# Decays kept in the chunk's frame, with query decays on GpSimd and a listed order: a retention, mixing and gated kernel

## The chip, the cores and the metric

The kernel runs on one core of a Trainium2 chip. The metric is the device time of one execution in microseconds; below 381.7 us stands for the kernel before. A core has TensorE (PE in the profile) for matrix products into PSUM, VectorE (DVE), ScalarE (ACT) and GpSimd (POOL) for work on elements, SyncE (SP), which here only issues transfers, and DMA engines between HBM and SBUF, the core's own memory. PSUM has eight banks of 512 float32 words in each of 128 partitions. Each engine works through its own list of instructions in order and waits at semaphores for the others.

## What is computed

Three layers follow each other on batch 2, sequence 768. The first is retention with 8 heads of 64, a state that decays by gamma at each step:

```python
gamma = 1.0 - 2.0 ** (-5.0 - np.arange(H, dtype=np.float32))
for t in range(S):
    state = gamma[None, :, None, None] * state + np.einsum('bhd,bhe->bhde', k[:, :, t], v[:, :, t])
    y[:, :, t] = scale * np.einsum('bhd,bhde->bhe', q[:, :, t], state)
```

The second takes its result as x (768 tokens of 512 features) and mixes tokens with two 768 x 768 matrices:

```python
theta = x @ w_theta
zr, zi = x * np.cos(theta), x * np.sin(theta)
u = x + einsum('ts,bsd->btd', w_tok_r, zr) + einsum('ts,bsd->btd', w_tok_i, zi)
x = u + np.maximum(u @ w_ch, 0.0)
```

The third is a gated layer: h = gelu(x @ w_in), a normalized half of it mixed over tokens by w_sg, multiplied into the other half, and projected back by w_out, with x added.

## The kernel before

The sequence is cut into chunks of 128 tokens: 6 for each batch, 12 in all, numbered i, with c the number within the batch. In `retention(i)` PE makes the scores of keys and queries of a chunk (8 small products), DVE multiplies them by the causal mask, PE makes the outer products of keys and values (8), which DVE adds to a running state, and the attend: state times query, and values times masked scores, into one PSUM bank. Decays are taken apart into powers. Values are multiplied by gamma to the minus t, with t counted from the start of the sequence (`dk`, one column for each chunk and head; ACT for the first eight chunks, DVE for the other four). The result is multiplied by gamma to the t, divided by the root of 64 (`dq`, one table of 256 KB for each chunk, loaded each time). DVE does that on the way out of PSUM, at L554. With these powers the state itself needs no decay.

All wide products are made in float32r in three terms: a number is split into a large part (ACT, a copy that rounds, L310) and the remainder (DVE, a subtraction, L316), and `terms3` issues large by large, remainder by large, large by remainder, for each of the pieces that are summed. Weights come as 1 MB blocks of float64 bits, which ACT (one pass, L369) and DVE (a shift and two combines, L378 and L389) turn into float32 ahead of the split. They land in one of two `raw` tiles.

`theta(i)` makes x @ w_theta in two halves with one weight block each, brings the angle into range, takes sine and cosine on ACT, transposes x with PE (`turn`, L648) and multiplies (L656) into the tile z, which is split too. `mix_main` and `mix_rest` are the token-mixing products. `channels`, `up_v`, `up_u`, `gate_tile` and `finish` follow once both batches are mixed.

Nothing is issued where it stands. Each piece of work becomes an `Op` with an engine, a duration by a formula, what it reads and writes, and a due time. `Plan.schedule` then builds the order greedily: of the work that could start first on an engine, the one with the smallest due time, with tiles and banks handed out as they come free. In the beginning PE has little to do, and up to ninety optional `keep_warm` operations, each one product of the identity matrix with itself, are taken where PE would otherwise stand idle.

All loads are issued by SP:

```python
dma(512, lambda: nc.sync.dma_start(out=ap(load[i, 0]), in_=qkv[b, c, 0]), ...)   # L413, queries and keys
dma(512, lambda: nc.sync.dma_start(out=ap(load[i, 1]), in_=qkv[b, c, 1]), ...)   # L424, keys and values
dma(256, lambda: nc.sync.dma_start(out=ap(dq), in_=dqs[c]), ...)                 # L485, query decays
```

They share eight semaphores in turn, so the issue of one transfer waits until the one eight places before it has landed.

Of the kernel before, what the change touches and what calls it, by code (L numbers as in the profile page):

```python
# [10 lines left out]
F32 = mybir.dt.float32  # L11
# [11 lines left out]
N = B * NCH  # L23

# [36 lines left out]
class Plan:  # L61
# [3 lines left out]
    BEGIN = {"PE": 5.2, "ACT": 2.0, "DVE": 2.0, "POOL": 1.3, "SP": 0.7}  # L65
# [28 lines left out]
    def schedule(self, look):  # L94


        engines = {o.eng: self.BEGIN.get(o.eng, 0.0) for o in self.ops}

        free = {of: [0.0] * n for of, n in self.room.items()}
        rank, level = {}, {}  # L100
        for k, o in enumerate(self.ops):
            o.missing, o.out = len(o.deps), []
            level[o] = max([o.lev, *(level[d] for d in o.deps)])
            rank[o] = k
            for d in o.deps:
                d.out.append(o)
        for o in self.ops:

            if o.eng == "SP" and o.out and not o.deps:
                level[o] = min(level[x] for x in o.out)  # L110
        for k, o in enumerate(sorted(self.ops, key=lambda o: (level[o], rank[o]))):
            o.pos = k
        use = {of: np.zeros(len(self.ops) + 1, np.int64) for of in self.room}
        for b in {b for o in self.ops for b in o.bufs}:
            b.todo = sorted(u.pos for u in b.users)
            b.first = b.todo[0]
            use[b.of][b.first : b.todo[-1] + 1] += 1
        for of, u in use.items():
            assert u.max() <= self.room[of], f"{of}: {u.max()} at {int(u.argmax())}"
        ready = {e: [] for e in engines}  # L120
        for o in self.ops:
            if not o.missing:
                ready[o.eng].append(o)
        state = {"port": 0.0, "dma": 2.1, "first": 0}
        done = [False] * (len(self.ops) + 1)

        def earliest(o):
            t = max(engines[o.eng], o.at, o.prio - (C["PA"] if o.eng == "PE" else C["AHEAD"]))
            if o.port:
                t = max(t, state["port"])  # L130
            o.spots = []
            more = {}
            for b in o.bufs:
                if b.base is not None:
                    continue
                n = more[b.of] = more.get(b.of, 0) + 1
# [1063 lines left out]
```

## Time and profile before

| | |
|---|---|
| median of 3 runs | 381.7 us (381.68 to 381.8) |
| span of the profiled execution | 381.1 us |
| PE busy | 374.7 us, 98% |
| DVE, ACT, POOL busy | 274.0, 175.0, 4.3 us |
| DMA | 41.96 MB, 110 GB/s over the span |
| TensorE's granted clock | 0.999 in the mean |

The profile is of one execution, whose span from the first to the last instruction is 381.1 us; the measured time holds 0.6 us more. A busy PE means that some product is under way. It does not tell whether the product is of use, and products overlap, so a mean duration is longer than the step from one to the next. Where an engine stood idle, the row says how long and which event ended it.

### The profile page before, as it was taken

The numbers are of one execution on the slowest core, as the hardware profiler recorded it, in microseconds if no ns is written. First come the engines' busy times: TensorE is split into PE (matmuls) and PEld (weight loads), VectorE is DVE, ScalarE is ACT, GpSimd is POOL, SyncE is SP. The second block draws the span as 40 slices with busy tenths as digits, with TensorE's granted clock in tenths as the row PEclk, the third lists the DMA queues.
The fourth block names the chain that finished last, engine by engine and source line by source line (L and its number), as shares of the span: only waits on it lengthen the run. The fifth ranks groups of instructions, "written<-read, shape, count | busy, mean of one in ns | idle before, by whom it ended". The sixth has DMA issues, their size and how long they took to land.

```text
span 381.1 us, 5873 instructions
## 1 busy us (share of the span) xinstructions
PE 374.7 (98%) x2422; PEld 318.4 (84%) x2422; DVE 274.0 (72%) x408; ACT 175.0 (46%) x292; POOL 4.3 (1%) x10
## 2 busy tenths in 40 slices
PE   7999999999999999999999999999999999999996
PEld 7877888878988978788998888888888888998885
DVE  1798999997977597869816685899899864544222
ACT  3677988563345335465313443595775711110000
POOL 1000000000000000003000000000000000000000
PEclk9999999999999999999999999999999999999999
DMA  7999553453435603029000160000000000000223
GB/s 258 411 407 407 208 191 110 144 223 132 165 114 192 248 2 113 0 101 352 4 2 2 31 244 2 1 0 0 2 0 1 2 1 0 2 2 35 103 89 106
DMA packets 11931, 41.96 MB, mean 110 GB/s; under 512 B 1536, under 2 KB 2560, under 8 KB 9472
## 3 DMA queue, kind: packets, MB, share of 16 engines
q1 hardware_dynamic: 11904, 41.58, 29.5%
q8 instruction: 19, 0.31, 0.3%
q14 instruction: 8, 0.07, 0.0%
HBM read 38.43 MB, written 3.15 MB: 109 GB/s over the span
## 4 chain that ended last, share of the span: by engine, by line
PE 93%; DMA 5%; SPq 0%; DVE 0%; issue 0%
PE b L290 92%; DMA b<-qkv 5%; PE b L648 1%; DVE b L1027 0%; SPq L424 0%; SPq L441 0%; SPq L413 0%
## 5 line engine op out<-in xcount | busy, mean ns | idle before, releaser
L290 PE MATMUL b<-b,b 128*128 128x512 f32 (+2 forms) x1788 | 332.6, 352 | 0.0
L290 PEld LDWEIGHTS b<-b,b 128*128 128x128 f32 (+1 forms) x1788 | 277.5, 183 | 47.0 <-issue 2.4
L310 ACT ACTIVATE b<-b 128x1024 fp32r<-128x1024 f32 (+1 forms) x64 | 53.2, 859 | 66.7 <-DVE b L975 38.2
L316 DVE TENSOR_TENSOR b<-b,b 128x1024 fp32r<-128x1024 f32 (+1 forms) x64 | 59.3, 955 | 9.7 <-ACT b L310 9.5
L389 DVE SCALAR_TENSOR_TENSOR b<-b 128x1024 int32<-128x1024 int32 x38 | 46.5, 1224 | 1.5 <-ACT b L369 0.5
L310 ACT ACTIVATE b<-xa 128x512 fp32r<-128x512 f32 x24 | 14.6, 626 | 22.9 <-DVE xa L777 9.9
L369 ACT ACTIVATE b<-b 128x1024 f32<-128x1024 f32 x19 | 21.8, 1155 | 3.6 <-DMA b<-wts 3.6
L290 PEld LDWEIGHTS b<-b 64*128 64x128 f32 (+1 forms) x352 | 17.3, 164 | 7.0 <-issue 2.8
L290 PE MATMUL b<-b 64*128 64x128 f32 (+1 forms) x352 | 20.5, 258 | 2.1 <-DMA b<-qkv 2.1
L457 DVE TENSOR_TENSOR b<-b,causal 128x512 f32<-128x512 f32 x24 | 15.7, 684 | 8.2 <-PE b L290 8.2
L316 DVE TENSOR_TENSOR b<-xa,b 128x512 fp32r<-128x512 f32 x24 | 16.2, 687 | 6.2 <-ACT b L310 6.0
L789 ACT ACTIVATE b<-b 128x512 f32<-128x512 f32 x24 | 13.8, 590 | 14.7 <-PE b L290 14.7
L475 ACT ACTIVATE b<-b,dk 128x64 f32<-128x64 f32 x64 | 16.1, 336 | 8.7 <-DMA b<-qkv 8.7
L968 DVE SCALAR_TENSOR_TENSOR b<-b,gcol,brow 128x512 f32<-128x512 f32 x12 | 9.0, 751 | 12.7 <-PE b L290 12.7
L813 DVE SCALAR_TENSOR_TENSOR b<-b,b 128x512 f32<-128x512 f32 x24 | 15.9, 678 | 2.9 <-ACT b L807 2.8
L807 ACT ACTIVATE b<-b 128x512 f32<-128x512 f32 x24 | 14.7, 629 | 6.2 <-DVE b L797 6.1
L797 DVE SCALAR_TENSOR_TENSOR b<-b,b 128x512 f32<-128x512 f32 x24 | 15.5, 672 | 1.9 <-ACT b L789 1.9
L604 ACT ACTIVATE b<-b 128x512 int32<-128x512 f32 x12 | 7.1, 594 | 19.9 <-PE b L290 19.9
L990 DVE TENSOR_TENSOR b<-b,xa 128x512 f32<-128x512 f32 x8 | 5.5, 690 | 14.2 <-PE b L290 14.2
L310 ACT ACTIVATE b<-xb 128x512 fp32r<-128x512 f32 x12 | 7.3, 628 | 17.5 <-DVE xb L735 9.9
L378 DVE TENSOR_SCALAR b<-b 128x1024 int32<-128x1024 int32 x19 | 13.1, 691 | 2.9 <-DMA b<-wts 2.7
L656 DVE TENSOR_TENSOR b<-b,b 128x1024 f32<-128x1024 f32 x12 | 14.6, 1220 | 0.8 <-ACT b L639 0.4
(51 smaller groups left out, 168.9 us busy)
## 6 DMA issues: line engine op xcount, KB each, us to landing
b<-wts SPq DMA_DIRECT2D x19, 1024.0 KB, 5.0
b<-qkv SPq DMA_DIRECT2D x24, 512.0 KB, 8.4
b<-dqs SPq DMA_DIRECT2D x12, 256.0 KB, 9.2
out<-b SPq DMA_DIRECT2D x11, 256.0 KB, 2.0
b<-wsg SPq DMA_DIRECT2D x9, 256.0 KB, 7.5
brow<-bvec SPq DMA_DIRECT2D x1, 384.0 KB, 7.7
out<-b SPq DMA_DIRECT2D x2, 128.0 KB, 1.7
dk<-decays SPq DMA_DIRECT2D x1, 24.0 KB, 3.4
```

Source lines behind the costliest of these rows:

```text
L290: nc.tensor.matmul(out=o, lhsT=l, rhs=r, start=start, stop=stop)
L310: act(words, lambda: A.activation(out=hi(), in_=src(), func=AF.Copy), prio=prio, r=r, **k)
L316: lambda: E.tensor_tensor(out=lo(), in0=src(), in1=hi().bitcast(F32), op=ALU.subtract),
L369: lambda: A.activation(out=words(1).bitcast(F32), in_=words(1).bitcast(F32), func=AF.Copy, scale=REBIAS),
L389: lambda scalar=scalar, op=op: V.scalar_tensor_tensor(out=words(0), in0=words(1), scalar=scalar, in1=words(0), op0=op, op1=ALU.bitwise_or,),
L457: V.tensor_tensor(out=ap(at[i])[:, h * 512 : (h + 1) * 512].rearrange("p (n t) -> p n t", n=NP), in0=ap(sc[h]).rearrange("p (n t) -> p n t ...
L475: A.activation(out=v, in_=v, func=AF.Copy, scale=dk[:, c, h : h + 1])
L656: V.tensor_tensor(out=z2, in0=ap(tp)[:, None, :].to_broadcast([P, 2, 512]), in1=z2, op=ALU.mult)
L789: lambda: A.activation(out=ap(s), in_=ap(t), func=AF.Square),
L797: lambda: V.scalar_tensor_tensor(out=ap(s), in0=ap(s), scalar=1.0 / GA, in1=ap(t), op0=ALU.add, op1=ALU.mult),
L807: lambda: A.activation(out=ap(s), in_=ap(s), func=AF.Tanh, scale=GA * GC),
L813: lambda: V.scalar_tensor_tensor(out=ap(o), in0=ap(s), scalar=1.0, in1=ap(t), op0=ALU.add, op1=ALU.mult),
```

## The change

Decays move into the frame of the chunk, with t counted from 1 to 128 in each. One table `dec` holds the query decays (512 columns), the value decays of the 8 heads and gamma to the 128 for the state. It is loaded once, and the twelve loads of `dqs` and the one of `dk` are gone. Queries are now multiplied by their decays ahead of the scores, in place: by DVE for chunk 0, by GpSimd for the other eleven (`weigh`). The state is multiplied by gamma to the 128 from chunk to chunk: in the copy itself after a batch's first chunk, by GpSimd after the four next (`shrink`). The result leaves PSUM without a multiply. ACT copies it to x and takes the large part, both from the bank, and DVE takes the remainder from the bank. All value decays are on ACT.

PSUM is one tile of eight banks, and the mask is one DVE instruction over two banks. Three weight blocks (both of theta, and the third of the token weights) land in the space of x tiles that are still empty, instead of in a `raw` tile. Chunk 0's keys and values are issued by ACT. The greedy planner is replaced by a list, `ORDER`, that gives the order of all operations; due times no longer matter. A pass over the list computes start times with changed constants, and identity products are put in where that pass has gaps of more than 0.25 us before 34 us.

```diff
-    BEGIN = {"PE": 5.2, "ACT": 2.0, "DVE": 2.0, "POOL": 1.3, "SP": 0.7}
+    BEGIN = {"PE": 4.2, "ACT": 2.3, "DVE": 1.4, "POOL": 2.0, "SP": 0.8, "SPA": 0.8}
+    FLY = 8
...
-    def schedule(self, look):
+    def schedule(self, order):
...
+        for o in (self.ops[k] for k in order):
+            t = max([engines[o.eng], *(d.end + (self.LAT if d.eng != o.eng else 0.0) for d in o.deps)])
...
+ORDER = [
+    56, 58, 59, 57, 62, 60, 85, 61, 89, 84, 63, 112, 65, 86, 67, 90, 64, 114, 66, 91, 87, 68, 0, 88,
...
-    dk = const.tile([P, NCH, H], F32, name="dk")
+    dec = const.tile([P, 512 + H + NP], F32, name="dec")
+    dq, dk, gone = dec[:, 0:512], dec[:, 512 : 512 + H], dec[:, 512 + H :]
...
+    homes = {
+        W_THETA: (xb.rearrange("p n b t -> p (n b t)"), [("x", b, c, d) for b in range(B) for c in (4, 5) for d in range(NP)]),
+        W_THETA + 1: (xa[1].rearrange("p n t -> p (n t)"), [("x", 1, c, d) for c in range(4) for d in range(NP)]),
+    }
+    homes[W_MAIN + 2] = homes[W_THETA + 1]
...
-            lambda: nc.sync.dma_start(out=ap(load[i, 1]), in_=qkv[b, c, 1]),
+            lambda: (nc.scalar if i == 0 else nc.sync).dma_start(
+                out=ap(load[i, 1]), in_=qkv[b, c, 1]
+            ),
...
+        def weigh():
+            (V if i < C["QD"] else G).tensor_tensor(
+                out=ap(qk)[:, 0:512], in0=ap(qk)[:, 0:512], in1=dq, op=ALU.mult
+            )
...
+            a, b = sorted(x.base for x in sc)
+            V.tensor_tensor(
+                out=ap(at[i]).rearrange("p (h n t) -> p h n t", h=2, n=NP),
+                in0=banks.rearrange("p (b n t) -> p b n t", b=8, n=NP)[:, a : b + 1 : b - a],
...
-        dma(
-            256,
-            lambda: nc.sync.dma_start(out=ap(dq), in_=dqs[c]),
...
+            def shrink():
+                G.tensor_tensor(
+                    out=state_next.rearrange("p (n d) -> p n d", n=NP),
+                    in0=grown.rearrange("p (n d) -> p n d", n=NP),
+                    in1=gone[:, :, None].to_broadcast([P, NP, D]),
+                    op=ALU.mult,
+                )
...
+        act(
+            512,
+            lambda: A.activation(out=x_chunk(i), in_=xp3(), func=AF.Copy),
...
-            lambda: V.tensor_tensor(
-                out=x_chunk(i),
-                in0=ap(xp).rearrange("p (n t) -> p n t", n=NP),
-                in1=ap(dq).rearrange("p (n t) -> p n t", n=NP),
-                op=ALU.mult,
...
+            if done < WARM and gap > 0.25:
+                idle = [k for k in range(8) if used.get(k, 0.0) <= done and k not in [b.base for b in o.bufs]]
+                keep_warm(idle[0], int(gap / 0.24))
```

How the order changes is shown at three places. Names are tiles, with `ident` for the identity matrix and `b` and `banks` for SBUF buffers and PSUM.

PE, from the attend of chunk 0 to the second chunk's. Before, `b0` and `b2` hold queries and keys of chunks 0 and 1, `b1` and `b5` their keys and values:

```order
L290 MATMUL b23_164<-b1_99 64x64 x8
L290 MATMUL b25_175<-b14_131,b1_99 64x128 x8
L290 MATMUL b26_187<-ident_64 128x128
L290 MATMUL b28_191<-ident_64 128x128
...
L290 MATMUL b45_236<-ident_64 128x128
L290 MATMUL b47_241<-b5_107 64x64 x8
L290 MATMUL b48_251<-b2_101,state1_82 64x128 x8
L290 MATMUL b48_251<-b24_173,b5_107 64x128 x8
```

After, from the scores of chunk 0 to the second theta product; here `b1` and `b2` are the keys and values of chunks 0 and 1, `b3` and `b4` the queries and keys of chunks 1 and 2:

```order
L283 MATMUL banks_63<-b0_96 128x128 x8
L283 MATMUL banks_63<-ident_64 128x128 x7
L283 MATMUL banks_63<-b1_98 64x64 x8
L283 MATMUL banks_63<-b9_138,b1_98 64x128 x8
L283 MATMUL banks_63<-ident_64 128x128
...
L283 MATMUL banks_63<-b19_204,b2_101 64x128 x8
L283 MATMUL banks_63<-ident_64 128x128 x8
...
L283 MATMUL banks_63<-b23_231,b5_108 64x128 x8
L283 MATMUL banks_63<-ident_64 128x128 x2
L283 MATMUL banks_63<-b27_266,b25_247 128x512 x2
```

Identity products stand in four groups of 7, 1, 8 and 2 behind the first scores, where before 17 in a row stood behind the first attend; scores, outer product and attend of chunk 2 now all stand ahead of the first theta product.

SP's queue from its start, before:

```order
L413 DMA b0_96<-qkv 128x1024
L441 DMA dk_80<-decays 128x48
L424 DMA b1_99<-qkv 128x1024
L413 DMA b2_101<-qkv 128x1024
L356 DMA b3_103<-wts 128x2048
L485 DMA b4_105<-dqs 128x512
L424 DMA b5_107<-qkv 128x1024
L356 DMA b6_109<-wts 128x2048
```

And after:

```order
L424 DMA b0_96<-qkv 128x1024
L455 DMA dec_80<-decays 128x524
L435 DMA b2_101<-qkv 128x1024
L424 DMA b3_103<-qkv 128x1024
L424 DMA b4_105<-qkv 128x1024
L364 DMA xb_87<-wts 128x2048
L435 DMA b5_108<-qkv 128x1024
L364 DMA xa1_86<-wts 128x2048
```

The table is second and eleven times as large as the one that stood there; chunk 0's keys and values have left the queue, the first weight stands behind three chunks' queries and keys, and no `dqs` load is left.

GpSimd behind the constants. Before, its list held only two small operations late in the kernel, which halve a column and a row. After, it begins with:

```order
L468 TENSOR_TENSOR b3_103<-b3_103,dec_80 128x512
L468 TENSOR_TENSOR b4_105<-b4_105,dec_80 128x512
L530 TENSOR_TENSOR state0_82<-grown_81,dec_80 128x256
L468 TENSOR_TENSOR b12_173<-b12_173,dec_80 128x512
L468 TENSOR_TENSOR b24_244<-b24_244,dec_80 128x512
L530 TENSOR_TENSOR state1_83<-grown_81,dec_80 128x256
L468 TENSOR_TENSOR b34_304<-b34_304,dec_80 128x512
```

Each 128x512 stands ahead of a chunk's scores, and each 128x256 ahead of the attend of the chunk that reads that state.

## Rows read from the trace of the kernel before

**Rows 1.** The page: busy times and shares, and the chain that ended last

```profile
PE 374.7 (98%) x2422; PEld 318.4 (84%) x2422; DVE 274.0 (72%) x408; ACT 175.0 (46%) x292; POOL 4.3 (1%) x10
PE 93%; DMA 5%; SPq 0%; DVE 0%; issue 0%
```

**Rows 2.** Timeline of PE, head: start, us, operation, records, idle before

```profile
5.02 1.16 PE L290 MATMUL b<-b 64*128 64x128 f32 x16
6.11 1.83 PE L290 MATMUL b<-ident 128*128 128x128 f32 x14
8.99 1.78 PE L290 MATMUL b<-b 64*128 64x128 f32 x32 [1.04 <-DMA b<-qkv]
10.59 1.04 PE L290 MATMUL b<-b,b 128*64 128x128 f32 x16
11.57 4.06 PE L290 MATMUL b<-ident 128*128 128x128 f32 x34
15.56 0.69 PE L290 MATMUL b<-b 128*64 128x64 f32 x16
16.18 1.09 PE L290 MATMUL b<-b,state 64*64 64x128 f32 x16
17.20 1.09 PE L290 MATMUL b<-b,b 128*64 128x128 f32 x16
18.78 1.16 PE L290 MATMUL b<-b 64*128 64x128 f32 x16 [0.49 <-DMA b<-qkv]
19.88 0.66 PE L648 MATMUL b<-ident,xa 128*128 128x128 f32 x4
20.37 1.06 PE L290 MATMUL b<-ident 128*128 128x128 f32 x8
22.01 1.78 PE L290 MATMUL b<-b 64*128 64x128 f32 x32 [0.59 <-DMA b<-qkv]
23.72 0.50 PE L290 MATMUL b<-b,b 128*128 128x512 f32 x1
```

**Rows 3.** Stretch: us, busy (x) of PE, PEld, DVE, ACT, POOL, PEclk, DMA share, GB/s

```profile
240.00:260.00 20.00, 20.00 (x90) 16.58 (x89) 17.95 (x41) 14.95 (x24) 0.00 (x0) 1.00 0.00 0
```

**Rows 4.** Timeline of SP's queue: issues 9, 11 and 15

```profile
4.99 0.63 SPq L413 DMA_DIRECT2D b<-qkv  x1
...
7.59 0.33 SPq L424 DMA_DIRECT2D b<-qkv  x1
...
13.32 0.33 SPq L485 DMA_DIRECT2D b<-dqs  x1
```

**Rows 5.** Stretches of the head, with DMA in the last columns

```profile
3.50:5.50 2.00, 2.00 (x18) 1.88 (x18) 0.00 (x0) 0.00 (x0) 0.00 (x0) 1.00 0.84 167
...
10.00:22.00 12.00, 10.93 (x146) 9.81 (x143) 9.98 (x13) 7.35 (x18) 0.00 (x0) 1.00 1.02 408
```

**Rows 6.** Groups by line and shape: busy us, mean ns, idle before

```profile
L290 PE MATMUL b<-b,b 128*128 128x512 f32 x1140 | 265.4, 392 | 0.0
L389 DVE SCALAR_TENSOR_TENSOR b<-b 128x1024 int32<-128x1024 int32 x38 | 46.5, 1224 | 1.5 <-ACT b L369 0.5
L316 DVE TENSOR_TENSOR b<-b,b 128x1024 fp32r<-128x1024 f32 x31 | 37.7, 1239 | 0.9 <-ACT b L310 0.7
...
L310 ACT ACTIVATE b<-b 128x1024 fp32r<-128x1024 f32 x31 | 34.0, 1111 | 28.5 <-PE b L290 20.5 <-DVE b L656 4.3 <-DVE b L389 3.7
...
L604 ACT ACTIVATE b<-b 128x512 int32<-128x512 f32 x12 | 7.1, 594 | 19.9 <-PE b L290 19.9
...
L554 DVE TENSOR_TENSOR xa<-b,b 128x512 f32<-128x512 f32 x8 | 5.5, 686 | 1.9 <-PE b L290 1.9
```

**Rows 7.** Timeline of ACT: the first chunk's value decays

```profile
7.66 2.02 ACT L475 ACTIVATE b<-b,dk 128x64 f32<-128x64 f32 x8 [5.60 <-DMA b<-qkv]
```

**Rows 8.** Timelines of DVE and of GpSimd near 178 us

```profile
178.56 1.85 DVE L316 TENSOR_TENSOR b<-b,b 128x1024 fp32r<-128x1024 f32 x1
...
178.09 2.54 POOL L1086 TENSOR_SCALAR brow<-brow 128x768 f32<-128x768 f32 x1
```

More of the change, by code (lines that the diff above doesn't have):

```diff
@@ L92, in op @@
         return o
-    def schedule(self, look):
-        engines = {o.eng: self.BEGIN.get(o.eng, 0.0) for o in self.ops}
+    def schedule(self, order):
+        engines = dict(self.BEGIN)
         free = {of: [0.0] * n for of, n in self.room.items()}
[L100 to L106, printed above, removed]
-        for o in self.ops:
[L109 to L128, printed above, removed]
@@ L180, in schedule @@
             else:
-                o.end = t + o.dur
+                engines[o.eng] = o.end = t + o.dur
             if o.port:
-                state["port"] = o.end
-            done[o.pos] = True
-            while done[state["first"]]:
-                state["first"] += 1
+                port = o.end
             for b in o.bufs:
-                last = b.todo[-1]
-                b.todo.remove(o.pos)
-                now = b.todo[-1] if b.todo else -1
-                use[b.of][now + 1 : last + 1] -= 1
-                if not b.todo:
-                    free[b.of][b.base] = max(u.end for u in b.users)
@@ L194, in schedule @@
-            for x in o.out:
-                x.missing -= 1
-                if not x.missing:
-                    x.at = max(d.end + (self.LAT if d.eng != x.eng else 0.0) for d in x.deps)
-                    ready[x.eng].append(x)
-            order.append(o)
-        rank = {o: k for k, o in enumerate(order)}
-        return sorted(order, key=lambda o: (o.start, rank[o]))
-C = dict(TC=13, LATE=90, AHEAD=60, LM=28, LT=9, LR=16, LW=15, LRW=15, PEL=0.1, DVEL=0.1, ACTL=0.7, CHP=5, SGP=10, RW2=0, PA=25, DEL=6, RS=3.8, LEAD=40, TH=-8, WARM=34.0, NWARM=90, FA=8, LEAD1=5)
+                todo[b] -= 1
@@ new lines, in schedule @@
+                last[b] = max(last.get(b, 0.0), o.end)
+                if not todo[b]:
+                    free[b.of][b.base] = last[b]
+        assert math.inf not in [x for room in free.values() for x in room]
+        rank = {k: n for n, k in enumerate(order)}
+        return [self.ops[k] for k in sorted(order, key=lambda k: (self.ops[k].start, rank[k]))]
+C = dict(TC=13.26, LATE=79.43, AHEAD=65.28, LM=28.32, LT=9.09, LR=20.66, LW=14.3, LRW=7.12, PEL=0.1, DVEL=0.06, ACTL=0.83, CHP=38.15, SGP=4.68, RW2=0, PA=37.2, DEL=5.73, RS=2.59, LEAD=38.54, TH=-5.54, WARM=33.56, NWARM=90, FA=12, QD=1, WLP=(), ZLP=(), XLP=(), LEAD1=6.04)
```

245 lines of the change are left out of this document (127 added, 118 removed), and 45 rows, old and new, of the table ORDER.

## Prediction

> **What bounds the kernel now.** I read the shares first. PE is busy for 98% of the span and makes up 93% of the chain that ended last [rows 1]. A busy PE is not yet a useful one, so the second view is PE's own timeline over the first 24 us [rows 2]. It shows when real products start, and where the order has put in products with the identity matrix that only keep the engine running. The pieces without use are:
>
> - 5.02 us until the first product with data;
> - 2.88 us from 6.11 to 8.99 (identity products, then a wait for a DMA);
> - 3.99 us from 11.57 to 15.56 (17 identity products, each in two records);
> - 0.49 us ahead of 18.78;
> - 1.64 us from 20.37 to 22.01.
>
> That makes 14.0 us. After 22 us no wait for data is left: a later stretch of 20 us holds 90 wide products in 20.00 us [rows 3], 0.222 us each, and no kind of product is slower than its own steady step. The rest of PE's time is work that the change does not touch. It has the same 1140 products of 512 columns, the same 456 of 256, and the same small ones. So the end can come earlier only by part of the 14.0 us, and later by any wait that appears behind 22 us. The tail, one DVE addition and one store, stays as it is.
>
> What holds the head up is DMA. The SP queue lets eight transfers fly, so an issue that ends a wait dates the landing of the transfer eight places before it [rows 4]. The first queries and keys land at 4.99 us, the first keys and values at 7.59, the second ones at 13.32. From 3.5 to 5.5 us the engines move 167 GB/s, and 408 GB/s from 10 us on [rows 5]. So 0.48 MB are missing there, 1.2 us of transfer. Just then the 24 KB table of key decays goes through, in rows of 192 bytes, and nothing else is ready behind it.
>
> **The change part by part.**
>
> *Loads.* Twelve query-decay loads of 256 KB and the table of 24 KB go; one table of 264 KB comes, second on SP's queue. Chunk 0's keys and values move to ACT's queue, beside SP's first. SP's other loads each move up past two or three removed ones. Most of the twelve were hidden already, since PE waits for no load after 22 us, and I cost them at nothing. In the head it counts.
>
> *First product.* Before, the scores of chunk 0 waited for its queries and keys alone (4.99, start 5.02). Now DVE multiplies the queries by the table first, so they wait for both. The table lands at the earliest 4.99 + 264 KB at 408 GB/s = 4.99 + 0.66 = 5.65. If the second half-megabyte is as late as before, it lands at 7.59 + 0.66 = 8.25. Between them: if ACT's queue fills half of the 0.48 MB gap, 0.24 MB of its 0.52 MB cost nothing and the rest 0.7 us, so 5.65 + 0.7 = 6.4, which I take. DVE's multiply of 512 takes 0.69 [rows 6], and a hand-over 0.1 (7.59 to 7.66 from landing to ACT's start [rows 4, 7]). First scores: 7.2 (6.4 to 9.0), against 5.02.
>
> *Identity products.* Eighteen stand behind the first scores in the new order (7, 1, 8 and 2). They run whether needed or not: 18 x 3.99/17 = 4.2 us. Those ahead of the scores lie in the wait.
>
> *Work ahead of the first wide product.* Three scores (1.1 each), three outer products (0.55), a first attend (0.98), two later ones (1.02 + 1.09 each) and one turn (0.49) make 10.7 us by the starts in [rows 2]. Before, it was two outer products and two attends, 8.0 us. So the first theta product can start at 7.2 + 10.7 + 4.2 = 22.1.
>
> *Does its data come by then?* The first theta weight has 3.76 MiB in its queue up to its own end; the load that ended at 3.27 MiB before landed at 13.32 [rows 4], so half a MiB later is 14.6, or 13.4 with the gap filled. Then ACT 1.13, DVE 2 x 1.22, ACT 1.13, DVE 1.24 [rows 6] give 20.5 at the latest, with 1.6 us to spare. Values of chunk 2 (4.26 MiB, 15.9) are faded by ACT in 2.02 [rows 7] behind that weight's first pass: 17.9, needed at 19. The second theta weight (5.26 MiB) lands by 18.4 in the same way, is split by 24.4 and due at 27.8.
>
> *GpSimd.* Query decays of chunks 1 to 11 and eight state decays go to GpSimd, ahead of the scores and attends. No row shows a GpSimd operation with two inputs. The nearest, one input of 768, took 2.54 us [rows 8]: 1.7 us for 512, or 3.4 if a second input doubles it. Below 1.7 it would only be hidden better. I take 1.7, the scaled row. For chunk 1: queries land at 10 to 10.7, decayed by 12.4, and PE comes to these scores at 7.2 + 5.0 = 12.2. So a wait of about 0.3 us, up to 3.7 at 3.4 us an operation, as chunk 2's stands behind it. The Trainium skill, GPSIMD Engine Reference, section 3.1, puts tensor_tensor at about 2.6 cycles an element at 1.2 GHz; by that 512 would be an estimated 1.1 us and this wait nothing. No run here shows it yet.
>
> *DVE and ACT.* DVE loses twelve multiplies of 0.69 (8.2 us) and four fades (2.7); the mask in one instruction saves almost nothing. ACT gains twelve copies out of PSUM at 0.59 and four fades at 2.02, 15.2 us. Neither is PE's path as long as the cover holds. DVE: from the first theta weight to the remainder of the first z tile the new order has 5 shifts, 10 combines, 5 weight or z remainders, 5 masks and 2 z multiplies of 1024, 11 operations of 512 and 5 of 256 (0.42 by the same slope): 39.9 us. PE has 38.7 us of theta and retention in that stretch and starts at 22.1 where DVE starts at about 14.5. So the cover is 6 us at its end, and about 4 us at its thinnest, halfway. ACT has 66.7 us of work up to the fourth token weight's large part; from 6.4, with some 3 us of waits, it is done near 76, and PE wants it (with DVE's 1.24 behind) at 80: a cover of 3 us.
>
> *Entries.* A wide product behind small ones starts with 0.11 us more (0.50 against 0.39 [rows 2, 6]); the new order has 16 such places for 12: +0.45.
>
> **The sum.** Without use before: 14.0. After: 7.2 + 4.2 + 0.3 = 11.7, and 0.45 for entries: 12.15. The difference is -1.9 us. The profiled execution's span is 381.1 and the median 381.7, so 0.6 us lie around the span; carried over, the median becomes 379.8.
>
> **The rivals.**
>
> *B: the table gates the head.* If the gap is not filled, the scores start at 9.0 and the sum is 9.0 + 4.2 + 0.3 + 0.45 = 13.95, no gain: 381.6. For it: one wait for one load has become one for two loads and a DVE operation. Against: the gap in [rows 5] is there to be filled, and ACT's queue is free.
>
> *C: GpSimd holds DVE.* In the trace a DVE subtraction of 1024 from two SBUF tensors took 1.85 us beside GpSimd's 2.54 us operation, and 1.24 elsewhere [rows 6, 8], 0.6 us held. In the stretch where the cover is 4 us the new order has 5 query and 3 state decays: 5 x 1.7 + 3 x 0.85 = 11 us of GpSimd. Held for 0.6 us each, DVE loses 4.9 us; held for all of them, 11 us. From 4 us on, PE waits. Of DVE's work there between 0.55 and 0.77 reads two SBUF tensors; with 0.7 of 11 us it loses 7.7, PE 3.7: 383.5, slower. Against it: masks, differences and z multiplies read PSUM, and the order can put GpSimd beside them. The Trainium skill, SBUF — State Buffer, section "SBUF: two separate sides", calls the shared pair an exclusive lock that the loser waits for during the whole instruction. The row agrees in kind (1.85 for 1.24), and by the rule taken at every operation the time would be C's or worse.
>
> *D: ACT becomes the bound* near 60 to 85 us. Its cover is 3 us, and it must also wait for PE and for DVE to release a bank. With 5 us of such waits PE loses 2: 381.8.
>
> *E: the best head.* Table at 5.65, no wait: 6.4 + 4.2 + 0.45 = 11.05, 378.7.
>
> **How the numbers follow.** Forecast A with its shades towards E 0.57, B 0.17, C 0.18, D 0.08. A ends under the limit almost always; B and D end near no change. Two tenths of a per cent, 0.76 us, is about what a measurement can tell here. Faster 0.58, same 0.19, slower 0.23. The range takes in E (378.7, less 0.3 for a GpSimd wait or entries that don't come) and C: 378.4 to 383.6. It leaves out a head with GpSimd at 3.4 us and a full hold together.
>
> **What would show it.** Right: first scores near 7.2, first wide product near 22, identity products still running, no PE wait after 22 us above some tenths. DMA moves over 300 GB/s from 3.5 to 5.5. Wrong: first scores at 9 (B); DVE operations of 1.24 us stretched to 1.8 or more and PE waiting for DVE between 25 and 60 us (C); PE waiting for ACT's large parts or for banks near 60 to 85 us (D); GpSimd's multiply far above 1.7 us. If PE waits behind 100 us, the searched order itself fails, which I gave no share of its own.

## The result

The changed kernel takes 385.85 us in the median (385.44 to 386.1), against 381.69 us for the kernel before. The ratio is 1.0103, 95% interval 1.0085 to 1.0121: about one per cent slower. The prediction was 379.8 us with a range of 378.4 to 383.6, so the sign is wrong and the time lies above the range.

The profiled execution after has a span of 383.7 us. From its page, the busy times and the chain that ended last, answering to [rows 1]:

```profile
PE 374.7 (98%) x2414; PEld 317.8 (83%) x2414; DVE 263.2 (69%) x381; ACT 184.0 (48%) x336; POOL 28.3 (7%) x29
PE 92%; DVE 3%; ACT 2%; DMA 1%; issue 1%; SPq 0%; DVEq 0%
```

PE is as busy as before. New is that 5% of the chain now runs through DVE and ACT, where it had none. PE's own timeline of the head, answering to [rows 2] (start, us, operation, records, idle time before and what ended it):

```profile
7.18 1.16 PE L283 MATMUL banks<-b 64*128 64x128 f32 x16 [0.39 <-DVE b L468]
8.28 1.83 PE L283 MATMUL banks<-ident 128*128 128x128 f32 x14
10.03 0.69 PE L283 MATMUL banks<-b 128*64 128x64 f32 x16
...
11.53 0.49 PE L283 MATMUL banks<-ident 128*128 128x128 f32 x2
11.94 1.78 PE L283 MATMUL banks<-b 128*64 128x64 f32 x32
...
17.37 2.05 PE L283 MATMUL banks<-ident 128*128 128x128 f32 x16
19.36 0.69 PE L283 MATMUL banks<-b 128*64 128x64 f32 x16
...
22.02 0.71 PE L283 MATMUL banks<-ident 128*128 128x128 f32 x4
22.48 1.63 PE L283 MATMUL banks<-b,b 128*128 128x512 f32 x6
```

The head is nearly what was forecast: first scores at 7.18 (forecast 7.2), first wide product at 22.48 (22.1). What was not forecast are PE's waits, which before had none behind 22 us. L601 is the remainder of a chunk's result, L478 the mask, L579 the copy of a result to x. Engine and line, what it waited for, us in total, times, longest:

```profile
PE banks L283 <- DVE b L601: 1.7, 2, 1.3
PE banks L283 <- DVE b L478: 1.4, 1, 1.4
PE banks L283 <- DVE state L262: 1.3, 1, 1.3
PE banks L682 <- ACT xb L579: 0.6, 1, 0.6
PE banks L283 <- DVE b L468: 0.4, 1, 0.4
```

The waits for L262 and L468 lie ahead of the first scores. The others lie behind the first wide product: 1.31 us at 27.48, 1.40 at 50.50, 0.61 at 52.67, 0.41 at 135.67, in sum 3.73 us. The first of them in PE's timeline:

```profile
27.48 1.43 PE L283 MATMUL banks<-b,b 128*128 128x512 f32 x5 [1.31 <-DVE b L601]
```

These four are what the experiments are about.

### The profile page after: what moved, and what is told of

Read it like the earlier page. It is cut to its first block, busy times and chain, and to the rows that moved or that the text cites. A ratio compares the mean times of both kernels' runs of the same rounds, so it can differ in the third digit from the quotient of the medians.

```text
span 383.7 us, 5857 instructions
## 1 busy us (share of the span) xinstructions
PE 374.7 (98%) x2414; PEld 317.8 (83%) x2414; DVE 263.2 (69%) x381; ACT 184.0 (48%) x336; POOL 28.3 (7%) x29
## 4 chain that ended last, share of the span: by engine, by line
PE 92%; DVE 3%; ACT 2%; DMA 1%; issue 1%; SPq 0%; DVEq 0%
PE banks L283 90%; DMA dec<-decays 1%; DVE xa L395 1%; PE banks L682 1%; ACT b L303 1%; DVE xb L395 1%; DVE b L478 1%; ACT xb L579 0%; DVE b L601 0%; ACT xa L375 0%; ACT b L593 0%; ACT b L496 0%; DVE b L468 0%; DVE xb L384 0%; ACT xa L579 0%
## 5 line engine op out<-in xcount | busy, mean ns | idle before, releaser
L283 PE MATMUL banks<-b,b 128*128 128x512 f32 (+2 forms) x1788 | 333.6, 352 | 1.7 <-DVE b L601 1.7
L283 PEld LDWEIGHTS banks<-b,b 128*128 128x128 f32 (+1 forms) x1788 | 277.6, 183 | 49.7 <-DVE b L601 2.5
L303 ACT ACTIVATE b<-b 128x512 fp32r<-128x512 f32 (+1 forms) x61 | 50.8, 847 | 90.8 <-DVE b L1010 39.7
L309 DVE TENSOR_TENSOR b<-b,b 128x512 fp32r<-128x512 f32 (+1 forms) x61 | 57.3, 950 | 22.4 <-ACT b L303 15.7
L496 ACT ACTIVATE b<-b,dec 128x64 f32<-128x64 f32 x96 | 24.0, 336 | 4.0 <-DMA dec<-decays 3.9
L283 PEld LDWEIGHTS banks<-b 64*128 64x128 f32 (+1 forms) x352 | 17.1, 164 | 6.3 <-issue 3.2
L283 PE MATMUL banks<-b 64*128 64x128 f32 (+1 forms) x352 | 20.3, 258 | 1.8 <-DVE b L478 1.4
L832 DVE SCALAR_TENSOR_TENSOR b<-b,banks 128x512 f32<-128x512 f32 x24 | 15.8, 680 | 8.6 <-ACT b L824 8.6
L478 DVE TENSOR_TENSOR b<-banks,causal 128x1024 f32<-128x1024 f32 x12 | 14.7, 1222 | 7.4 <-PE banks L283 7.4
L468 POOL TENSOR_TENSOR b<-b,dec 128x512 f32<-128x512 f32 x11 | 17.3, 1576 | 23.5 <-DMA b<-qkv 23.5
L848 DVE SCALAR_TENSOR_TENSOR b<-b,banks 128x512 f32<-128x512 f32 x24 | 15.9, 677 | 0.2
L384 DVE TENSOR_SCALAR b<-b 128x1024 int32<-128x1024 int32 x16 | 11.3, 711 | 3.8 <-DMA b<-wts 3.8
```

What stands on the lines that cost most here:

```text
L283: nc.tensor.matmul(out=o, lhsT=l, rhs=r, start=start, stop=stop)
L303: act(words, lambda: A.activation(out=hi(), in_=src(), func=AF.Copy), prio=prio, r=r, **k)
L309: lambda: E.tensor_tensor(out=lo(), in0=src(), in1=hi().bitcast(F32), op=ALU.subtract),
L468: (V if i < C["QD"] else G).tensor_tensor(out=ap(qk)[:, 0:512], in0=ap(qk)[:, 0:512], in1=dq, op=ALU.mult)
L478: V.tensor_tensor(out=ap(at[i]).rearrange("p (h n t) -> p h n t", h=2, n=NP), in0=banks.rearrange("p (b n t) -> p b n t", b=8, n=NP)[:, a ...
L496: A.activation(out=v, in_=v, func=AF.Copy, scale=dk[:, h : h + 1])
```

## The experiments

In each diff the lines with a minus are those of the kernel named at its start. Ratios are to the kernel before, timed on the same chip at the same time.

**1. The kernel before again.** No edit.

> The kernel before, unchanged, for a second trace of it. All runs so far lie 1.73 us above their own span, and the spans of the kernel before lie between 379.6 and 381.4 us with 380.1 as the commonest, so the traced execution with its span of 381.1 was one of the long ones. Theory T (its length differs in the head, where PE waits for loads): with a span near 380.1 the three waits of PE for loads before 24 us (1.04, 0.49 and 0.59, sum 2.1 us) come to 1.0 to 1.3 us in sum, and PE from 24 us on is as before. Rival (the difference lies in the steady part or behind the last product): the waits still sum to 2.0 us or more.

Measured: 381.75 us, span 380.0. PE's head:

```profile
5.40 1.47 PE L290 MATMUL b<-b 64*128 64x128 f32 x16
6.80 1.83 PE L290 MATMUL b<-ident 128*128 128x128 f32 x14
9.07 1.78 PE L290 MATMUL b<-b 64*128 64x128 f32 x32 [0.44 <-DMA b<-qkv]
...
18.30 1.16 PE L290 MATMUL b<-b 64*128 64x128 f32 x16
...
20.88 1.78 PE L290 MATMUL b<-b 64*128 64x128 f32 x32
22.58 1.66 PE L290 MATMUL b<-b,b 128*128 128x512 f32 x6
```

Two of the three waits for loads in [rows 2] are gone and the third is 0.44 us: 0.44 instead of 2.12 in sum. The first scores come 0.38 later and the first wide product 1.14 us earlier. In 57 runs timed beside the experiments the span of the kernel before lies between 379.4 and 381.4 us, median 380.1. Its time is 1.7 to 1.8 us above its span in every one of them, and so is the changed kernel's in its four. By that the execution behind the prediction, with its span of 381.1, was one of the long ones and took about 382.8 us, which none of the three timed runs did (381.68 to 381.8). "0.6 us lie around the span" set the span of one execution against the time of another. From the first wide product to PE's last one, both executions take 354.4 us, so the difference lies in the head: theory T holds, though the wait that is left, 0.44 us, is under its 1.0 to 1.3. In this execution the time without use ahead of the wide products is 5.40 + 2.27 + 3.99 + 0.99 = 12.65 us, not 14.0.

**2. The mask as two instructions** (on the changed kernel).

```diff
-            a, b = sorted(x.base for x in sc)
-            V.tensor_tensor(
-                out=ap(at[i]).rearrange("p (h n t) -> p h n t", h=2, n=NP),
-                in0=banks.rearrange("p (b n t) -> p b n t", b=8, n=NP)[:, a : b + 1 : b - a],
-                in1=causal[:, None, None, :].to_broadcast([P, 2, NP, P]),
-                op=ALU.mult,
-            )
+            for h, x in enumerate(sorted(sc, key=lambda x: x.base)):
+                V.tensor_tensor(
+                    out=ap(at[i])[:, h * 512 : (h + 1) * 512].rearrange("p (n t) -> p n t", n=NP),
+                    in0=ap(x).rearrange("p (n t) -> p n t", n=NP),
+                    in1=causal[:, None, :].to_broadcast([P, NP, P]),
+                    op=ALU.mult,
+                )
```

> The changed kernel with the causal mask as two DVE instructions of 512, one for each bank, instead of one instruction over two banks. Theory M (the one instruction names a stretch of PSUM from the lower to the higher of its banks, and waits for, and is waited for by, work in the banks between): PE's waits of 1.40 us ahead of the outer product at 50.50 and of 0.61 us ahead of the turn at 52.67 both go; each mask pair costs DVE 2 x 0.69 - 1.22 = 0.15 us more, three of them ahead of the wait at 27.5, which grows by up to 0.45. Time 385.85 - 2.0 + 0 to 0.45 = 383.8 to 384.3 us. Rival (the list itself puts the outer product and the turn too early, whatever the mask names): both waits stay, and the time is 385.8 to 386.3 us.

Measured: 383.19 us, ratio 1.0029 (1.0017 to 1.0041). 2.66 us are gone, more than the 2.0 us that were expected at most. The two waits are 2.0 of them; in the traces PE's end came 2.2 us earlier, and 0.3 us more went behind it. The wait at 27.48 did not grow, as it might have; the rest stays open. First DVE and PE of the changed kernel around 47 us:

```profile
45.35 1.23 DVE L395 SCALAR_TENSOR_TENSOR b<-b 128x1024 int32<-128x1024 int32 x1
49.22 1.23 DVE L478 TENSOR_TENSOR b<-banks,causal 128x1024 f32<-128x1024 f32 x1 [2.64 <-PE banks L283]
```

```profile
45.90 1.16 PE L283 MATMUL banks<-b 64*128 64x128 f32 x16
...
48.01 1.09 PE L283 MATMUL banks<-b,b 128*64 128x128 f32 x16
50.50 0.69 PE L283 MATMUL banks<-b 128*64 128x64 f32 x16 [1.40 <-DVE b L478]
```

The scores of chunk 6 end at 47.06, yet its mask starts at 49.22, when the attend of chunk 5 has ended at 49.10. It does not need that attend. The scores lie in banks 1 and 5, the attend writes bank 4, and the semaphores of the built program say the same: this mask waits for PE's last product into bank 4 and for ACT's read of bank 2, and ACT's next copy, out of bank 2, waits for the mask. The outer product behind it wants the bank that the mask frees. This order is part of the program as it was built; no run says that the chip asks for it. DVE with two instructions:

```profile
47.14 1.29 DVE L478 TENSOR_TENSOR b<-banks,causal 128x512 f32<-128x512 f32 x2 [0.50 <-PE banks L283]
```

It starts with the end of the scores, and both waits, at 50.50 and at 52.67, are gone from the list of PE's waits:

```profile
PE banks L283 <- DVE b L601: 1.8, 2, 1.3
```

**3. Two instructions only where the banks aren't neighbours.** The one instruction stands for the eight chunks whose banks are neighbours, the two for chunks 5, 6, 9 and 11.

```diff
             a, b = sorted(x.base for x in sc)
-            V.tensor_tensor(
...
+            if b - a == 1:
+                V.tensor_tensor(
...
+                return
+            for h, x in enumerate(sorted(sc, key=lambda x: x.base)):
+                V.tensor_tensor(
...
```

> The changed kernel with the mask as two instructions only for the four chunks (5, 6, 9 and 11) whose two banks of scores are not neighbours; the other eight, with neighbouring banks, keep the one instruction. Theory M in its narrow form (the one instruction is ordered against work in the banks that lie between its two): as with all twelve masks apart; no wait at 50.5 and 52.7, time 382.7 to 383.4 us, beside 383.19. Rival (one instruction over two banks costs in any case, because it starts only when both banks are ready): at least a part of the 2 us stays, 384 us or more.

Measured: 383.15 us, ratio 1.0038 (1.0024 to 1.0052). The same gain, so the price was that of the strided reach over banks in between, not of one instruction for two banks. Theory M in its narrow form is shown. Of the four masks, chunk 6's is the one that both waits hung on.

**4. Two query decays left out** (on the changed kernel).

```diff
         def weigh():
+            if i in (3, 4):
+                return
             (V if i < C["QD"] else G).tensor_tensor(
```

> The changed kernel without the query decays of chunks 3 and 4 (two GpSimd multiplies of 512, at 21.4 and 24.0 us, left out, so the result of these two chunks lacks them). Theory L (a GpSimd operation and a DVE operation that reads two SBUF tensors hold each other off): DVE's two combines at 22.3 and 24.6, 2.32 and 2.20 us long, shrink to 1.22 to 1.24 each, the remainder behind them ends 2.0 us earlier, and PE's wait of 1.31 us at 27.48 goes. Time 384.4 to 384.7 us. Rival (DVE's list is too long up to there even without GpSimd): the combines keep their length or the wait stays above 0.8 us, time 385.4 to 385.9 us.

Measured: 384.61 us, ratio 1.0066 (1.0050 to 1.0082). What they did, in the changed kernel, DVE first and then GpSimd:

```profile
21.13 1.23 DVE L309 TENSOR_TENSOR b<-xb,b 128x1024 fp32r<-128x1024 f32 x1
22.27 4.55 DVE L395 SCALAR_TENSOR_TENSOR xa<-xa 128x1024 int32<-128x1024 int32 x2
26.75 0.68 DVE L601 TENSOR_TENSOR b<-banks,b 128x512 fp32r<-128x512 f32 x1
```

```profile
9.04 2.50 POOL L468 TENSOR_TENSOR b<-b,dec 128x512 f32<-128x512 f32 x2 [7.18 <-DMA b<-qkv]
...
21.41 2.09 POOL L468 TENSOR_TENSOR b<-b,dec 128x512 f32<-128x512 f32 x1 [7.59 <-DMA b<-qkv]
23.97 1.77 POOL L468 TENSOR_TENSOR b<-b,dec 128x512 f32<-128x512 f32 x1 [0.47 <-DMA b<-qkv]
```

A multiply takes GpSimd 1.25 to 1.29 us when DVE reads PSUM or nothing (two in 2.50 at 9.04). Beside DVE's subtraction at 21.13 and the combines behind it, it took 2.09 and 1.77, and the two combines took 4.55 us instead of 2.48. PE waited for the remainder (L601) that ended at 27.43. Without the two multiplies:

```profile
22.85 2.48 DVE L395 SCALAR_TENSOR_TENSOR xa<-xa 128x1024 int32<-128x1024 int32 x2
25.24 0.69 DVE L603 TENSOR_TENSOR b<-banks,b 128x512 fp32r<-128x512 f32 x1
```

The wait at 27.48 is gone. The one at 135.67 grew from 0.41 to 0.87 in that trace, and the time is 1.2 us shorter. Theory L holds.

**5. The same two decays held back** (on the changed kernel). Each waits for a DVE result by copying one column of it.

```diff
+    held = {}
+    scrap = const.tile([P, 2], I32, name="scrap")
...
+        held[k] = lambda: whole()[:, 0:1]
...
         def weigh():
+            if i == 3:
+                G.tensor_copy(out=scrap[:, 0:1], in_=held[1]())
+            if i == 4:
+                G.tensor_copy(out=scrap[:, 1:2], in_=ap(wp[1][1], I32)[:, 0:1])
             (V if i < C["QD"] else G).tensor_tensor(
```

> The changed kernel, in which GpSimd's query decays of chunks 3 and 4 are held back by a copy of one column each: the first reads a word that DVE's second combine of the second theta weight writes, the other a word of that weight's remainder. So neither multiply can lie beside those. Theory L (GpSimd and DVE hold each other off): as without the two multiplies; combines of 1.22 to 1.24 us each at 22.3 and 23.5, no wait at 27.48, time 384.4 to 384.8 us. Rival (the two multiplies are needed as early as they ran): PE waits for them ahead of the scores at 28.8 or 31.5, time 385.3 to 386.5 us.

Measured: 384.17 us, ratio 1.0062 (1.0046 to 1.0079). Nothing is left out here, and the gain of experiment 4 is there, 0.2 us under what was expected. GpSimd's multiply now starts when the combines have ended, and is short again; DVE first, then GpSimd:

```profile
22.14 2.48 DVE L400 SCALAR_TENSOR_TENSOR xa<-xa 128x1024 int32<-128x1024 int32 x2
24.54 0.68 DVE L610 TENSOR_TENSOR b<-banks,b 128x512 fp32r<-128x512 f32 x1
```

```profile
24.69 0.18 POOL L474 COPY scrap<-xa 128x1 int32<-128x1 int32 x1 [10.99 <-DVE xa L400]
24.82 1.30 POOL L477 TENSOR_TENSOR b<-b,dec 128x512 f32<-128x512 f32 x1
```

**6. The second DMA queue, from both sides.** In the changed kernel SP issues chunk 0's keys and values again, third in its queue:

```diff
-            lambda: (nc.scalar if i == 0 else nc.sync).dma_start(
+            lambda: nc.sync.dma_start(
...
-            eng="SPA" if i == 0 else "SP",
+            eng="SP",
```

> The changed kernel with chunk 0's keys and values issued by SP, third in its queue behind the table, so that ACT issues no transfer. Theory Q (a program that uses a second engine's DMA queue pays for it outside of its span): what lies around the span falls from 1.7 us to the 0.6 us of the kernel before. The first scores stay near 7.2 (queries and table are still first and second) or come earlier, and the outer product of chunk 0 may come up to 0.7 us later. Time 384.7 to 385.4 us. Rival (the 1.1 us more around the span come from something else in the program): it stays at 1.7 us and the time is 385.8 to 386.5 us.

Measured: 385.84 us, ratio 1.0099 (1.0084 to 1.0114). And in the kernel before, ACT issues them:

```diff
-            lambda: nc.sync.dma_start(out=ap(load[i, 1]), in_=qkv[b, c, 1]),
+            lambda: (nc.scalar if i == 0 else nc.sync).dma_start(
+                out=ap(load[i, 1]), in_=qkv[b, c, 1]
+            ),
```

> The kernel before with only chunk 0's keys and values moved from SP's queue to ACT's. Theory Q: around the span lie 1.7 us instead of 0.6. The load lands earlier than 7.59, so the wait of 1.04 us ahead of 8.99 may go, and SP's loads behind it move up; the span is 380.0 to 381.1 us and the time 381.7 to 382.8 us. Rival (no cost of a second queue): around the span lie 0.6 us, time 380.6 to 381.7 us, which would be faster than before by the head's gain alone.

Measured: 381.05 us, ratio 0.9976 (0.9965 to 0.9987). Theory Q falls in both: the time stays 1.7 us above the span with one queue as with two. That 1.7 for 0.6 had only been the misreading of experiment 1. The move itself is worth 0.8 us in the kernel before, where PE waited for loads (0.44 to 2.12 us in the two traces of it, none here), and nothing that can be measured in the changed one, where the first scores moved by 0.34 us (7.18 to 7.52). Something is hidden there, though. Without the load on ACT's queue the table came earlier, and DVE's multiply of chunk 0's queries, which waits for it, started at 4.92 us for 6.44:

```profile
4.92 0.69 DVE L468 TENSOR_TENSOR b<-b,dec 128x512 f32<-128x512 f32 x1 [3.71 <-DMA dec<-decays]
```

So the queries were ready at 5.61, but PE was still on the seven identity products that stand ahead of the scores, its records 0.21 us apart up to 6.97, and began the scores at 7.52. Those 1.9 us of the head went to products without use, and no run here took these seven out.

**7. Three causes removed together** (on the changed kernel): experiments 2 and 5, and in the listed order one shift of a weight block is moved (shown in the old line breaks).

```diff
-    481, 344, 259, 362, 390, 221, 389, 261, 263, 345, 316, 482, 468, 222, 363, 483, 391, 361, 399,
+    481, 344, 259, 362, 390, 221, 389, 261, 263, 345, 316, 482, 222, 363, 483, 391, 361, 399,
...
-    293, 346, 485, 413, 366, 294, 292, 414, 469, 486, 232, 225, 367, 415, 473, 424, 416, 368, 748,
+    293, 346, 485, 413, 366, 294, 292, 414, 468, 469, 486, 232, 225, 367, 415, 473, 424, 416, 368, 748,
```

It is the shift (L384, operation 468) that the wait at 135.67 hung on. DVE in the changed kernel:

```profile
134.32 0.70 DVE L384 TENSOR_SCALAR b<-b 128x1024 int32<-128x1024 int32 x1 [3.83 <-DMA b<-wts]
134.93 0.69 DVE L601 TENSOR_TENSOR b<-banks,b 128x512 fp32r<-128x512 f32 x1
```

DVE stood 3.83 us ahead of a shift whose block had not landed, and the remainder that PE wanted stood behind it.

> Three edits on the changed kernel together: the mask as two instructions, the two query decays held back, and the shift of the weight block that PE's wait of 0.42 us at 135.67 hung on moved in DVE's list to just ahead of the combine that needs it, behind the remainder that it held up. If the waits found in the trace are independent of each other: 383.19 (two masks) - 1.35 - 0.44 = 381.4, so 381.1 to 381.9 us, and no wait of PE above 0.3 us after its first product with data. Rival (waits that were hidden behind these come up): 382.2 to 383.2 us.

Measured: 380.96 us, ratio 0.9977 (0.9968 to 0.9985). The list of PE's waits has none left behind its first product with data. The four waits were independent, no hidden one came up, and the time is 0.1 us under the range expected. The shift was not moved by itself, so its share is known from the trace alone (0.41 us).

**8. Without the identity products behind the first scores** (on the changed kernel).

```diff
-            if done < WARM and gap > 0.25:
+            if done < 5.0 and gap > 0.25:
```

> The changed kernel without the 18 identity products behind the first scores; the seven ahead of them stay. Theory V (DVE's conversion of the first theta weight sets the start of the first wide product: its remainder ended at 22.35, the product began at 22.48): PE's time saved ahead of the scores of chunk 2, up to 1.2 us, brings chunk 2's mask and so the conversion behind it in DVE's list forward by 0.8 to 1.2 us, the rest becomes waiting; time 384.6 to 385.1 us. Rival as the prediction counted (the 18 products cost their own 4.2 us): first wide product at 18.3, time near 381.7 us. Second rival (TensorE's granted clock falls when it is left idle): PEclk below 1.0 after 8 us, time above 385.9 us.

Measured: 383.42 us, ratio 1.0040 (1.0028 to 1.0052). PE:

```profile
9.86 1.09 PE L283 MATMUL banks<-b,b 128*64 128x128 f32 x16 [0.78 <-DVE b L478]
...
19.93 0.73 PE L283 MATMUL banks<-b,b 128*128 128x512 f32 x2 [1.19 <-ACT b L303]
21.18 1.21 PE L283 MATMUL banks<-b,b 128*128 128x512 f32 x4 [0.53 <-DVE b L309]
```

The 18 products take 4.6 us of PE, and their absence brought 2.4: neither the 1.2 of theory V nor all of it. The conversion came 1.2 us earlier, as theory V had it (its remainder starts at 19.91 for 21.13). But PE needn't wait for that remainder: its first two products take the large part alone, so it began at 19.93, 1.19 us after it was free, and waited again, 0.53 us, for the remainder. A wait of 0.78 us for the first mask, at 9.86, came up as well. The wait at 27.48 shrank to 0.70, the one at 135.67 grew to 0.99. The second rival is not borne out in this trace, whose granted clock is 1.00; two of the other four runs show 0.994 and 0.996 in the mean.

**9. Both, 7 and 8.**

> The three edits together (mask as two instructions, query decays of chunks 3 and 4 held back, one shift moved), and without the 18 identity products behind the first scores. Those 18 alone were worth 385.85 - 383.42 = 2.4 us, of which 0.6 was the wait at 27.5 growing shorter (1.31 to 0.70), which is gone here already. If the rest adds up: 380.96 - 1.8 = 379.1, so 378.8 to 379.7 us, first wide product near 20, then waits of 1 to 2 us in sum for the first theta weight. Rival (DVE's list, with 0.15 us more for each mask, takes the gain): 379.8 to 380.9 us.

Measured: 380.49 us (379.05 to 381.64), ratio 0.9952 (0.9936 to 0.9968), 1.4 us above what was expected. Busy times of PE, PEld, DVE, ACT and POOL, granted clock, DMA share and GB/s, of this kernel:

```profile
22.00:24.00 2.00, 2.00 (x9) 1.63 (x8) 1.97 (x3) 1.38 (x2) 0.45 (x2) 0.52 1.04 416
```

and of the one of experiment 8:

```profile
22.00:24.00 2.00, 2.00 (x12) 1.69 (x11) 1.97 (x2) 0.92 (x1) 1.42 (x1) 1.00 1.03 410
```

The granted clock is 0.52 of full speed from 22 to 24 us, so nearly all of that stretch is at the lower of its two levels, 1.2 GHz. PE had stood idle for 1.23 us ahead of 19.88 and for 0.52 ahead of 21.14. The dozen wide products that follow at 22.98 took 4.17 us, and 3.00 in experiment 7. Four of the six runs show such a clock (0.995 in the mean of the run); the two at 1.0 throughout took 379.05 and 379.67, which is the forecast. The waits alone don't decide it: the traced run of experiment 8 had almost the same two (1.19 and 0.53) and kept 1.00, and which executions lose the clock stays open.

**10. The theta conversion ahead of chunk 2's mask** (on experiment 9). Operation 116 is the mask of chunk 2, 1 to 4 and 6 the conversion of the first theta weight, 9 the shift of the second, 96 the remainder of chunk 1's result. The rest keeps its order.

```diff
-    113, 76, 92, 115, 7, 14, 140, 141, 116, 1, 2, 3, 4, 9, 117, 93, 168, 118, 95, 5, 121, 96, 8, 6,
+    113, 76, 92, 115, 7, 14, 140, 141, 1, 2, 3, 4, 116, 117, 93, 168, 118, 95, 5, 121, 8, 6, 9, 96,
```

> As the one before, and in DVE's list chunk 2's mask stands behind the shift and the two combines of the first theta weight instead of ahead of them, and this weight's remainder ahead of the second weight's shift. Theory V (DVE's conversion of that weight sets the start of the wide products): the conversion starts 1.4 us earlier, its remainder ends near 19.6, PE's waits there shrink to under 0.5 us in sum; 377.8 to 378.5 us. Rival (the weight has not landed by then, or PE now waits for chunk 2's mask): 378.6 to 379.5 us.

Measured: 379.11 us, ratio 0.9930 (0.9917 to 0.9942), the fastest of all: 0.7% under the kernel before, 6.7 us under the changed one. PE:

```profile
18.82 1.52 PE L274 MATMUL banks<-b,b 128*64 128x128 f32 x15 [0.17 <-DVE b L478]
21.25 1.43 PE L274 MATMUL banks<-b,b 128*128 128x512 f32 x5 [0.91 <-DVE b L601]
```

The waits for the theta weight are gone, but PE now waits 0.91 us for the remainder of chunk 1's result, which I had put behind, and 0.3 for the mask. So a part of the gain went into new waits, and the time is the rival's (378.6 to 379.5). The clock stayed at 1.0 in all five runs. In experiments 9 and 10 the time lies 1.7 to 2.9 us above the span, 2.0 in the median, where the kernel before has 1.7 beside them; why is open, and it makes these two times 0.3 us longer than their spans would say.

**11. The same with neighbouring masks in one instruction.**

> The fastest kernel so far (379.11: mask apart, two decays held back, one shift moved, no identity products behind the first scores, chunk 2's mask behind the first theta weight's conversion), with the masks over neighbouring banks as one instruction again. DVE is relieved of 8 x 0.15 = 1.2 us in sum, three of these eight ahead of PE's wait of 0.91 us at 21.25: that wait shrinks to 0.4 to 0.6 us and the time is 378.4 to 378.9 us. Rival (the halves let PE start earlier: attend begins with the first half of a mask): no gain, 379.0 to 379.5 us.

Measured: 379.42 us, ratio 0.9946 (0.9934 to 0.9959): no gain, as the rival had it. PE waits 0.78 us for the first mask here, and 0.23 + 0.16 where it is apart, because attend starts on the first half. The row where it is apart, and the one where it is not:

```profile
9.64 0.43 PE L274 MATMUL banks<-b,b 128*64 128x128 f32 x2 [0.23 <-DVE b L478]
```

```profile
10.20 1.09 PE L274 MATMUL banks<-b,b 128*64 128x128 f32 x16 [0.78 <-DVE b L479]
...
21.17 1.44 PE L274 MATMUL banks<-b,b 128*128 128x512 f32 x5 [0.98 <-DVE b L610]
```

But the rival's reason explains little. Only one head's product runs ahead on the half; the turn behind it starts at 12.81 us with the masks apart and at 12.78 with one instruction, and the first wide product at 21.25 and 21.17. What failed is the saving: the one instruction saves DVE 0.07 us and not 0.15, the remainder that PE waits for starts 0.08 us earlier (20.43 for 20.51), and that wait is 0.98 us for 0.91.

## Why the prediction was wrong, step by step

Two steps failed. The larger is a term that the sum put at nothing: behind the first wide product it has no wait of PE, and 3.73 us of waits stand there, 2.0 for the mask, 1.3 at a place where DVE's cover was thinner than counted, and 0.4 from the listed order. The other is the step from a span to a time, which gave the kernel before 1.35 us too much without use. The head itself came as forecast. With the waits taken out (experiment 7) the change is worth 0.9 us, 380.96 for 381.86.

**The account.** Against the ordinary execution of the kernel before (experiment 1) the span grew by 383.7 - 380.0 = 3.7 us; the medians of the times differ by 4.2, since the profiled execution is the shortest of four. Time without use ahead of the wide products: 7.18 and the four identity groups, 1.75 + 0.41 + 1.99 + 0.46 = 4.61, so 11.79 for 12.65, or -0.86. Waits behind that: +3.73. Entries were forecast at +0.45 and not measured. That makes 3.3; PE's end moved by 3.1, from 377.02 to 380.13, read from the last rows of PE in the traces of experiment 1 and of after:

```profile
369.68 7.34 PE L290 MATMUL b<-b,b 128*128 128x512 f32 x43
```

```profile
359.75 20.38 PE L283 MATMUL banks<-b,b 128*128 128x256 f32 x115
```

What is behind PE's last product grew from 3.0 to 3.6 us, which gives the rest; of that, the last stores took 2.1 us to land for 1.7, and why they did is open.

**What bounds the kernel now.** The sum of 14.0 us without use was right for the execution that was read, and 1.35 too high for the ordinary one. What failed is "0.6 us lie around the span": a span was set against the median of other runs, and the 1.1 us between 0.6 and the 1.7 measured since are the length of that execution. Read rightly, the forecast gain would have been 0.5 us. Two smaller readings were off and moved nothing in the sum. In the gap of [rows 5] the DMA engines were 84% busy, so it was slow transfer and not a lack of transfers that were ready: eight were issued by 4.2 us. And the work ahead of the first wide product before, "8.0 us", is 23.72 - 14.0 = 9.7 by [rows 2], with four scores and three outer products in it.

**Loads, first product, identity products, first wide product.** Right, and near their sizes. The table landed at 6.34 (forecast 6.4), the DMA engines moved 396 GB/s from 3.5 to 5.5 us where [rows 5] have 167, first scores came at 7.18, and the identity products took 4.61 us for the 4.2 forecast. So rival B and case E are out. That the products "run whether needed or not" is shown by experiment 8, with 2.4 us of the 4.6 as their price. The other 2.2 would have been waiting. "Those ahead of the scores lie in the wait" is right for the profiled execution, where PE still waits 0.39 us behind them, and not for that of experiment 6, where they set the start of the scores.

**The mask.** That "the mask in one instruction saves almost nothing" is the costliest line of the prediction: 2.66 us in experiment 2. The line looked at durations, 1.22 for 2 x 0.69, and not at what the instruction is ordered against. No rival had this.

**GpSimd.** The multiply takes 1.25 to 1.29 us alone, below the 1.7 taken. By the Trainium skill, GPSIMD Engine Reference, section 3.1, it was an estimated 1.1 us; that was nearer, and the measured number decides. No wait for chunk 1's decay came.

**DVE's cover and rival C.** The mechanism of C is there and its price was too high. DVE lost 1.1 + 1.0 us at 22.3 to 26.8, 1.1 at 61.07 and 0.7 at 75.25, with smaller pieces about 4.2 us in all, where C had 7.7; and PE lost 1.3 of it, where C had 3.7. Two of the places where DVE was held:

```profile
61.07 2.29 DVE L309 TENSOR_TENSOR b<-b,b 128x1024 fp32r<-128x1024 f32 x1
```

```profile
75.25 1.96 DVE L395 SCALAR_TENSOR_TENSOR b<-b 128x1024 int32<-128x1024 int32 x1
```

PE did not wait behind either. It waited at 27.48, where the prediction saw the cover still growing. Cover was counted from the first wide product to the end of the stretch and halfway; at 27.48 PE had used up the dozen wide products that two chunks' results give with the first theta weight, and wanted the remainder of the third, which DVE's list has behind both combines of the second weight. That is where the count of the cover failed: the thinnest place is at the first thing that stands behind a long piece in DVE's list, not in the middle. The Trainium skill, SBUF — State Buffer, section "SBUF: two separate sides", calls the ports that GpSimd and DVE share an exclusive lock in which the one that starts first keeps the pair. This trace agrees: the combine that started at 22.27, inside a multiply that ran to 23.50, ended at 24.59, 1.09 us after it; alone it takes 1.22.

**ACT, rival D.** ACT was not the bound. The wait of 0.61 us at 52.67 names ACT, but ACT's copy had itself waited 3.35 us for the mask, and experiment 2 removed it. ACT's cover near 60 to 85 us held: no wait of PE stands there.

**The searched order.** It got no share of its own. The wait at 135.67 (0.41 us) is its fault: it has a DVE instruction stand for a block that lands later than the list assumed. In part so is the lock: the list's own times put chunk 3's decay behind the combines, but an order within each engine holds nothing between engines, and the multiply ran when its load had landed.

## What to carry to other kernels

Before two instructions are merged into one, look at all that the merged one is ordered against: here one strided operand over banks 1 and 5 was made to wait for work in banks 2 and 4, and the saving of 0.07 us a mask (1.22 for 1.29) cost over two microseconds. Work moved to an engine that shares a path with a busy one wants a place where the other reads elsewhere, and a real dependence that keeps it there; a planned time doesn't. And take a second execution of the kernel before ahead of summing: spans differed by 2 us from run to run, which is as much as the whole forecast.

## What the runs showed that I had not expected

- GpSimd and DVE hold each other off in both directions: GpSimd's 1.29 us multiply became 1.77 to 2.24, and DVE's 1.22 us combine 1.96 to 2.32. DVE work on PSUM beside it kept its length (a mask of 1.23 us at 30.12 with a multiply of 1.29 at 30.30). The shift with a single SBUF input was held too, 1.51 us for 0.69 in experiment 5.
- With waits of 1.23 and 0.52 us close together in the head, PE's granted clock came down to 0.52 from 22 to 24 us in the traced run of experiment 9, and did not in that of experiment 8 with waits of 1.19 and 0.53. With the 18 identity products none of experiment 7's eleven runs shows a clock under 0.998, without them four of experiment 9's six show 0.995 and none of experiment 10's five. Their price in the changed kernel was 2.4 us.
- An attend can start on half a mask: the two smaller instructions, 0.07 us longer in sum, let PE start 0.56 us sooner than the one. It is done no sooner, though.
- The seven identity products ahead of the first scores can set the start of the head: in experiment 6 they ran until 7.5 us, and the data had been ready at 5.61.
